# Moving an 80-word pad in SBUF: the weights start 192 bytes past a multiple of 512, the moving operands stay on it

## The chip, the cores and the metric

The kernel runs on one core of a Trainium2 chip. The metric is the device time of one execution in microseconds (us), taken as the median over runs.

## What is computed

Linear attention with a decay, then two feed-forward layers. All inputs are float32.

```
for t in range(S):                       # B, H, S, D = 4, 8, 768, 48
    state = alpha[:, :, t, :, None] * state + k_t (outer) v_t
    y[:, :, t] = q_t @ state
x = y as 3072 tokens x 384
x = ((x @ w_a) * (x @ w_b)) @ w_out      # d_ff = 1536
h = x @ w_in                             # d_ff = 2048
out = (max(h, 0) + alpha2 * min(h, 0)) @ w_out2
```

## The kernel before, in words

Every large product is made of three TensorE matmuls on operands that are split into a high and a low float32r part (high x high, low x high, high x low). The helper `mm3` (lines 931, 932 and 934) issues them. A matmul has a stationary operand, which a weight load (LDWEIGHTS) brings into the array, and a moving operand, which streams through it. In `mm3` the stationary operand is always a 128 x 128 piece of a weight tile: 512 bytes of each partition. The moving operand is 512 columns (2048 bytes of each partition), in the first block of tokens of the first unit 256.

The tokens are worked on in six blocks of 512. In the first layer `up` fills PSUM tiles `pa` and `pb` (moving `x`), a product and a split make `gh` and `gl`, and `down` adds into `acc` (moving `gh`, `gl`). In the second layer the PSUM tile of `up` is `pi`, and the weight tiles are called `v`. Attention chunks, 24 of them, stand between these matmuls in the first half. For the first four chunks TensorE has little else to do, and it is kept busy with throwaway bf16 matmuls (`wp`, line 343).

The order of all instructions comes from a planner (`Graph`), which works with a table of costs and due times. It knows no addresses, and it writes the instructions out engine by engine ahead of time.

Weights come from HBM as 64-bit numbers into a slot of the pool `wpool` and are turned there into the two float32r halves by ScalarE and VectorE (`conv`, lines 409 to 453). For three of the units the low half is found by TensorE (lines 481 to 483, tile `cl`): there the stationary operands are the constant matrices `plus` (+1 on the diagonal) and `minus` (-1), and the converted weights are the moving operand. The second layer's weights go back to HBM after conversion (`w2d`) and are loaded again as `v` tiles when slots are free. Chunks 2 and 3 of the attention keep their inputs `ra` and `kq` in weight slots that are not in use yet; chunks 0 and 1, and all later ones, keep them in the pool `tp`.

Where a tile lies in its partition is fixed when the program is built: pools lie one after the other in the order in which they are opened, and each is as large as its tiles. These are the bytes at which they start in the program before, and what is left of that when it is divided by 512 (its residue):

| pool, tiles | before: first byte, residue | after: first byte, residue |
|---|---|---|
| const: plus, minus, mask, betaT | 1152, 128 | 1152, 128 |
| pad of 80 words | 2752, 192 (end of const) | 125632, 192 (behind wpool) |
| wpool: 20 slots of 6144 bytes (weights; `vg`; `ra`, `kq` of chunks 2 and 3) | 3072, 0 | 2752, 192 |
| xpool: x | 125952, 0 | 125952, 0 |
| cpool: c1, c2 | 158720, 0 | 158720, 0 |
| gpool: a_sb, ng, gh, gl, x2 | 171008, 0 | 171008, 0 |
| tp: ra | 195584 and 199744, 0 and 64 | the same |
| tp: kq, v, ks; pers: Z, As, heads | 203904 and on, 128 | the same |

Every slot of wpool is 12 x 512 bytes long, and every piece that `mm3` takes as stationary operand starts a multiple of 512 bytes into its slot, so each has the residue of the pool. The 64-column pieces of `v` and `vg` in the attention are 256 bytes long: those of `v` start at residues 128 and 384, those of `vg` at 0 and 256. The operand of the throwaway matmuls starts 4 bytes into `heads`, at residue 132.

Of the kernel before, what the change touches and what calls it, by code (L numbers as in the profile page):

```python
# [14 lines left out]
F32 = mybir.dt.float32  # L15
# [10 lines left out]
P = 128  # L26
# [13 lines left out]
PAD = 80  # L40
# [259 lines left out]
def body(tc, akq, v, vg, w_a, w_b, w_o1, w_in, w_o2, beta, out):  # L300
# [13 lines left out]
    with ExitStack() as ctx:  # L314
        ctx.enter_context(tc.manual_schedule())
        pool = lambda name, bufs=1, **k: ctx.enter_context(tc.tile_pool(name=name, bufs=bufs, **k))
        const, wpool, xpool = pool("const"), pool("wpool"), pool("xpool", 2)
        cpool, gpool, tp, pers = pool("cpool", 2), pool("gpool", 2), pool("tp", 2), pool("pers")
        dram = pool("dram", space=DRAM)
        ps_mm, ps_acc = pool("ps_mm", 2, space=PSUM), pool("ps_acc", space=PSUM)  # L320
# [5 lines left out]
        ident = plus.bitcast(F32)  # L326
        mask = const.tile([P, P], F32, name="mask")
        betaT = const.tile([P, F2], F32, name="betaT")
        const.tile([P, PAD], F32, name="pad")
        Z = pers.tile([P, BC, NJ, D], F32, name="Z")  # L330
        At = pers.tile([P, NC + 2 * NJ * D + NC], F32, name="As")
        heads = pers.tile([P, NJ, CH + 1], F32, name="heads")
# [922 lines left out]
```

## Time and profile before

| | |
|---|---|
| median of 3 runs | 932.51 us (932.1 to 932.53) |
| the profiled execution's own time | 932.32 us |
| its span on the core | 930.6 us |
| TensorE busy (matmul) | 925.4 us, 6585 matmuls |
| weight loads busy | 757.0 us, 6585 loads |
| VectorE busy | 560.5 us |
| ScalarE busy | 242.6 us |
| mean granted TensorE clock | 1.0 of full |

The span is the time from the first to the last instruction on the core; the rest of the profiled execution's time lies around it. Records of matmuls overlap, since one starts while the one before still drains, so the time that one matmul costs is read from start to start and not from its own length.

### The profile page before, as it was taken

The page shows a single profiled execution, that of the slowest core. Times are in us where ns is not written, and L with a number is a line of the kernel's source. Part 1 is how long each engine was busy: PE and PEld are TensorE (multiplying, and loading weights), DVE is VectorE, ACT ScalarE, POOL GpSimd, SP SyncE. Part 2 cuts the span into 40 slices and gives each one's busy share as a digit, 9 for nine tenths or more (in the row PEclk, how much of TensorE's full clock was granted, in tenths as well). Part 3 has the DMA queues.
Part 4 walks back from the last instruction along what each step waited for, and adds up shares of the span by engine and source line. Part 5 has one row for each costly group of instructions (what it writes and reads, how often), then busy time and mean ns, then how long its engine had stood idle before and what let it go on. Part 6 is the DMA issues. An engine that isn't in the chain of part 4 may idle for free.

```text
span 930.6 us, 15550 instructions
## 1 busy us (share of the span) xinstructions
PE 925.4 (99%) x6585; PEld 757.0 (81%) x6585; DVE 560.5 (60%) x855; ACT 242.6 (26%) x396; POOL 7.0 (1%) x34
## 2 busy tenths in 40 slices
PE   9999999999999999999999999999999999999998
PEld 7887888888888888888888888888888888888886
DVE  8999996777668866532232254555545545555544
ACT  3555433333323332212222211111211111111211
POOL 0000000000000000000000000000000000000000
PEclk9999999999999999999999999999999999999999
DMA  9971256676748754430265610200200200200000
GB/s 363 402 282 51 89 159 199 185 217 213 225 136 260 234 159 141 116 92 22 77 236 203 236 70 1 83 19 1 98 5 1 101 1 1 102 1 0 35 1 35
DMA packets 75237, 112.89 MB, mean 121 GB/s; under 512 B 38688, under 2 KB 48416, under 8 KB 75168
## 3 DMA queue, kind: packets, MB, share of 16 engines
q1 hardware_dynamic: 75024, 111.77, 36.2%
q8 instruction: 52, 0.85, 0.4%
q14 instruction: 17, 0.14, 0.1%
q10 hardware_dynamic: 144, 0.13, 0.0%
HBM read 78.97 MB, written 30.93 MB: 118 GB/s over the span
## 4 chain that ended last, share of the span: by engine, by line
PE 97%; DVE 1%; DMA 1%; issue 1%; ACT 0%; DVEq 0%; ACTq 0%
PE acc L931 13%; PE acc L934 12%; PE acc L932 12%; PE pi L931 7%; PE pi L932 7%; PE pi L934 7%; PE pa L931 6%; PE pb L931 5%; PE pa L932 5%; PE pa L934 5%; PE pb L932 5%; PE pb L934 5%; PE both L791 2%; PE both L630 1%; PE both L813 1%; PE both L798 1%
## 5 line engine op out<-in xcount | busy, mean ns | idle before, releaser
L955 ACT CAST gh<-ng 128x512 fp32r<-128x512 f32 x96 | 59.7, 622 | 326.0 <-DVE ng L1168 251.3
L1164 DVE TENSOR_SCALAR ng<-pi,betaT 128x512 f32<-128x512 f32 x96 | 72.1, 751 | 97.1 <-PE pi L934 96.2
L959 DVE TENSOR_TENSOR gl<-ng,gh 128x512 fp32r<-128x512 f32 x96 | 66.3, 690 | 84.8 <-ACT gh L955 84.8
L1062 DVE TENSOR_TENSOR a_sb<-a_sb,pb 128x512 f32<-128x512 f32 (+1 forms) x74 | 49.5, 669 | 111.7 <-PE pb L934 110.8
L931 PE MATMUL pi<-x,v 128*128 128x512 f32 x288 | 112.8, 392 | 0.0
L932 PE MATMUL pi<-x,v 128*128 128x512 f32 x288 | 112.1, 389 | 0.0
L931 PE MATMUL acc<-gh,v 128*128 128x512 f32 x288 | 112.0, 389 | 0.0
L932 PE MATMUL acc<-gh,v 128*128 128x512 f32 x288 | 112.0, 389 | 0.0
L934 PE MATMUL acc<-gl,v 128*128 128x512 f32 x288 | 112.0, 389 | 0.0
L931 PE MATMUL acc<-gh,wo 128*128 128x512 f32 (+1 forms) x222 | 86.9, 391 | 0.0
L931 PE MATMUL pa<-x,wa 128*128 128x512 f32 (+1 forms) x222 | 86.6, 392 | 0.0
L931 PE MATMUL pb<-x,wb 128*128 128x512 f32 (+1 forms) x222 | 86.5, 391 | 0.0
L932 PE MATMUL acc<-gh,wo 128*128 128x512 f32 (+1 forms) x222 | 85.3, 384 | 0.0
L934 PE MATMUL acc<-gl,wo 128*128 128x512 f32 (+1 forms) x222 | 85.2, 384 | 0.0
L932 PE MATMUL pb<-x,wb 128*128 128x512 f32 (+1 forms) x222 | 85.0, 384 | 0.0
L932 PE MATMUL pa<-x,wa 128*128 128x512 f32 (+1 forms) x222 | 85.0, 384 | 0.0
L934 PE MATMUL pi<-x,v 128*128 128x512 f32 x288 | 80.9, 389 | 0.0
L955 ACT CAST gh<-a_sb 128x512 fp32r<-128x512 f32 (+1 forms) x74 | 45.1, 609 | 131.9 <-DVE a_sb L1062 124.0
L1059 ACT COPY a_sb<-pa 128x512 f32<-128x512 f32 (+1 forms) x74 | 42.5, 574 | 137.4 <-PE pa L934 137.2
L1168 DVE SCALAR_TENSOR_TENSOR ng<-pi,ng 128x512 f32<-128x512 f32 x96 | 66.3, 691 | 3.1
L931 PEld LDWEIGHTS pi<-x,v 128*128 128x128 f32 x288 | 54.0, 188 | 13.7 <-DVE ng L1168 2.6
L932 PEld LDWEIGHTS acc<-gh,v 128*128 128x128 f32 x288 | 54.1, 188 | 11.3
(122 smaller groups left out, 1343.7 us busy)
## 6 DMA issues: line engine op xcount, KB each, us to landing
kq<-in_akq SPq DMA_DIRECT2D x24, 512.0 KB, 5.1
w2d<-ws SPq DMA_DIRECT2D x16, 768.0 KB, 4.1
v<-w2d SPq DMA_DIRECT2D x16, 768.0 KB, 5.2
x2d<-x SPq DMA_DIRECT2D x18, 512.0 KB, 3.8
x<-x2d SPq DMA_DIRECT2D x6, 1536.0 KB, 7.2
ra<-in_akq SPq DMA_DIRECT2D x24, 258.5 KB, 3.0
v<-in_v SPq DMA_DIRECT2D x24, 256.0 KB, 5.2
rs<-in_w_in SPq DMA_DIRECT2D x8, 768.0 KB, 6.4
```

The costliest lines, as they stand in the source:

```text
L630: nc.tensor.matmul(a[hs, i, j, :], kT()[ps, j, hs], qT()[ps, j, hs], start=True, stop=True, skip_group_check=True)
L791: nc.tensor.matmul(y_of(k, half(p), part_of(h)), s["v"][part_of(h), 2 * j + i, :], s["As"][part_of(h), i, j, :], start=first, stop=False, ...
L798: nc.tensor.matmul(y_of(k, slice(64 * p, 64 * p + D), part_of(h)), z[ps, j, :], qT()[ps, j, part_of(h)], start=False, stop=last, skip_grou ...
L931: nc.tensor.matmul(o, lh, rh, start=first and n == 0, stop=False)
L932: nc.tensor.matmul(o, ll, rh, start=False, stop=False)
L934: nc.tensor.matmul(o, lh, rl, start=False, stop=last and n == len(pairs) - 1)
L955: nc.scalar.copy(gq[idx][0], src())
L959: nc.vector.tensor_tensor(out=gl, in0=src(), in1=gh.bitcast(F32), op=ALU.subtract)
L1059: nc.scalar.copy(b["a"], ba["t"])
L1062: nc.vector.tensor_tensor(out=b["a"], in0=b["a"], in1=bb["t"], op=ALU.mult)
L1164: nc.vector.tensor_scalar(out=b["n"], in0=bh["t"], scalar1=0.0, scalar2=betaT[:, i : i + 1], op0=ALU.min, op1=ALU.mult)
L1168: nc.vector.scalar_tensor_tensor(out=b["n"], in0=bh["t"], scalar=0.0, in1=b["n"], op0=ALU.max, op1=ALU.add)
```

## The change

One line of the pools and one line of the tiles. The pad leaves the pool `const` and gets a pool of its own, `gap`, that is opened between `wpool` and `xpool`. So wpool moves down by 320 bytes, from residue 0 to residue 192, and everything from xpool on stays where it was. On every engine, and in the DMA queues, the same instructions stand in the same order with the same shapes.

```
-        const, wpool, xpool = pool("const"), pool("wpool"), pool("xpool", 2)
+        const, wpool, gap, xpool = pool("const"), pool("wpool"), pool("gap"), pool("xpool", 2)
...
-        const.tile([P, PAD], F32, name="pad")
+        gap.tile([P, PAD], F32, name="pad")
```

## Rows read from the trace of the kernel before

**Rows 1.** The page's first two parts: busy time by engine, and 40 slices.

```profile
PE 925.4 (99%) x6585; PEld 757.0 (81%) x6585; DVE 560.5 (60%) x855; ACT 242.6 (26%) x396; POOL 7.0 (1%) x34
PE   9999999999999999999999999999999999999998
PEclk9999999999999999999999999999999999999999
DMA  9971256676748754430265610200200200200000
```

**Rows 2.** The chain that ended last, by engine; then a piece of it (start, us, what).

```profile
PE 97%; DVE 1%; DMA 1%; issue 1%; ACT 0%; DVEq 0%; ACTq 0%
...
27.11 5.85 DMA ra<-in_w_a
```

**Rows 3.** Groups by shape (count | busy us, mean ns | idle): first and last 512-wide matmul groups, loads.

```profile
L931 PE MATMUL pi<-x,v 128*128 128x512 f32 x288 | 112.8, 392 | 0.0
...
L934 PE MATMUL pa<-x,wa 128*128 128x512 f32 x210 | 59.0, 389 | 0.0
L932 PEld LDWEIGHTS pi<-x,v 128*128 128x128 f32 x288 | 54.1, 188 | 11.1
```

**Rows 4.** Timeline of TensorE and its loads in the second layer (start us, length us).

```profile
701.23 0.19 PEld L931 LDWEIGHTS pi<-x,v 128*128 128x128 f32 x1
701.45 0.39 PE L931 MATMUL pi<-x,v 128*128 128x512 f32 x1
701.45 0.19 PEld L932 LDWEIGHTS pi<-x,v 128*128 128x128 f32 x1
...
705.53 0.39 PE L931 MATMUL pi<-x,v 128*128 128x512 f32 x1
```

**Rows 5.** Timeline of TensorE: 256-wide `mm3` matmuls, and the throwaway ones.

```profile
24.87 0.28 PE L932 MATMUL pa<-x,wa 128*128 128x256 f32 x1
24.98 0.28 PE L931 MATMUL pa<-x,wa 128*128 128x256 f32 x1
25.10 0.28 PE L932 MATMUL pa<-x,wa 128*128 128x256 f32 x1
25.22 0.28 PE L931 MATMUL pa<-x,wa 128*128 128x256 f32 x1
...
10.77 1.58 PE L343 MATMUL wp<-heads 128*128 128x256 bf16 x13
```

**Rows 6.** Timeline of TensorE: the low half of weights (stationary plus, minus).

```profile
30.37 0.33 PE L483 MATMUL cl<-wb,plus 128*128 128x384 f32 x1
30.54 0.28 PE L931 MATMUL pb<-x,wb 128*128 128x256 f32 x1
```

**Rows 7.** Timeline of TensorE: scores of the first four chunks.

```profile
9.19 1.16 PE L620 MATMUL A<-kq 48*128 48x128 f32 x16
...
14.23 1.16 PE L620 MATMUL A<-kq 48*128 48x128 f32 x16
...
21.30 1.16 PE L620 MATMUL A<-kq 48*128 48x128 f32 x16
...
27.37 1.16 PE L620 MATMUL A<-kq 48*128 48x128 f32 x16
```

**Rows 8.** Timeline of TensorE: stationary `v`, then stationary `vg`.

```profile
15.83 0.84 PE L778 MATMUL both<-As,v 128*64 128x128 f32 x12
16.50 0.83 PE L782 MATMUL both<-As,vg 128*64 128x128 f32 x12
```

**Rows 9.** One line's instructions, VectorE (duration ns min/median/max, first and last start).

```profile
L603 DVE TENSOR_TENSOR kq<-kq,ra x24: 1199/1218/1228, 6.6 to 408.2; 128x1024 f32<-128x1024 f32 x24
```

**Rows 10.** Busy time by engine in a stretch (PE, PEld, DVE, ACT, POOL), clock, DMA share.

```profile
40.00:100.00 60.00, 60.00 (x651) 49.75 (x651) 59.95 (x101) 32.34 (x48) 0.65 (x3) 1.00 0.50 185
```

**Rows 11.** DMA issues (count, KB each, median us from issue to landing).

```profile
kq<-in_akq SPq DMA_DIRECT2D x24, 512.0 KB, 5.1
...
v<-w2d SPq DMA_DIRECT2D x16, 768.0 KB, 5.2
...
ra<-in_akq SPq DMA_DIRECT2D x24, 258.5 KB, 3.0
```

## The prediction

> **What bounds the kernel now.** I read the page's first two parts first: TensorE is busy for 925.4 of 930.6 us, in nearly every slice, at the full granted clock (2.4 GHz) [rows 1]. Then the chain that ended last: 97% of it is TensorE, 1% DMA, 1% VectorE [rows 2]. So the time is a number of matmuls times what one costs from start to start, and the view for that is the timeline. In the second layer the same matmul of `pi` comes again after 705.53 - 701.45 = 4.08 us, and 18 matmuls (nine of `up`, nine of `down`) lie in between: 0.2267 us each [rows 4]. 512 columns at 2.4 GHz are 0.2133 us, so a beat is the streaming of the moving operand and 0.0133 us more. The reader should also see when the weight loads run: a load starts at the same 701.45 at which the matmul before its own starts, takes 0.19 us by its record, and is over before the next start [rows 4]; the loads' own row has 11.1 us of idle time before 288 loads, some 39 ns each [rows 3].
>
> How many beats there are: six groups of 288 and nine of 210 matmuls, 512 wide, of which rows 3 show the first and the last: 1728 + 1890 = 3618, and 3618 x 0.2267 = 820 us of the span. 108 more are 256 wide. One nanosecond on every wide beat is 3.6 us. I count 0.2%, 1.9 us, as what a measurement of this kernel can tell from no change; that is 0.5 ns a beat, about one cycle of the full clock. So the question is narrow: does a stationary operand at residue 192 cost one cycle per matmul or none?
>
> **The change part by part.** No instruction is added, removed or moved. Three kinds of access get another address: weight loads (every matmul of `mm3`), VectorE and ScalarE work on the weight slots, and DMAs into and out of them. The pad itself is never touched.
>
> *Weight loads, for themselves.* A 512-byte piece at residue 0 lies within one stretch of 512 bytes, at residue 192 across two. If the load grew longer, would the beat? The narrow matmuls answer that: 256 columns start every 0.12 us (24.98, 25.10, 25.22), each with a full 128 x 128 load of its own [rows 5]. So loads can follow each other every 0.12 us, against 0.2267 us in a wide beat: some 0.1 us of cover, more than if a load took 1.8 times as long. Where the cover is gone, in the 108 narrow matmuls, a load 10% longer would cost 108 x 0.012 = 1.3 us. I take 0 for both.
>
> *Weight loads, against the moving stream.* The other way in is that the load, which reads SBUF while the matmul before it streams, holds up that stream at some pairs of addresses. The kernel before already has such pairs. Scores: chunks 0 and 1 have both operands at residue 128, chunks 2 and 3, in weight slots, at residue 0; all four groups of 16 last 1.16 us [rows 7]. To the 0.01 us of the rows that is at most 0.01/16 = 0.6 ns a matmul. Attention: pieces of `v` at 128 and 384, of which every second straddles a multiple of 512, against pieces of `vg` at 0 and 256, which never do: 0.84 and 0.83 us for 12 [rows 8], at most 0.01/11 = 0.9 ns, and the first of `v` stands behind other work. Float32r: the matmul of line 483 has a stationary operand at residue 128 and a moving one at 0. From its start to the next is 30.54 - 30.37 = 0.17 us for 384 columns [rows 6]; on the line between the narrow beat of 0.12 and the wide one of 0.2267, both of residue 0 throughout, it would be 0.173. And the throwaway bf16 matmuls, with both operands at 132, a residue that is a multiple of 4 alone, run one every (1.58 - 0.28)/12 = 0.108 us for 256 columns, against 0.1067 of streaming [rows 5] (0.28 us being about the length of one record). Nothing here depends on the residue of the stationary operand. What the rows do not have is residue 192 itself (64 past a multiple of 128) in float32r. So the value is 0, and the bounds are 0 and 0.9 ns x 3618 = 3.3 us; below nothing I let only the collision rival in.
>
> *VectorE and ScalarE on weight slots.* VectorE is full from 40 to 100 us, 59.95 of 60 [rows 10], so work that became slower there would have no cover. But the product of line 603 works on `kq` in weight slots for chunks 2 and 3 and in tp, at residue 128, for the others, and all 24 lie between 1199 and 1228 ns [rows 9]. I take 0; the whole spread, 2.4% of the 60 us, gives the upper bound of 1.4 us.
>
> *DMAs.* Weights are loaded before they are needed, and the chain waits for one of them only once, 5.85 us at 27.11 [rows 2]; that is the one place without cover. Loads to other residues land after 5.1 us for 512 KB (`kq`) and 3.0 us for 258.5 KB (`ra`, whose tile is loaded from its middle), loads of weights after 5.2 us for 768 KB [rows 11]: 10.0, 11.6 and 6.8 ns per KB. A fixed part explains that order, but taken as if it all came from the address it bounds the wait at 5.85 x 11.6/6.8 = 10.0 us, 4.1 us more. I take 0, since a start-up share of each DMA is the plainer reading.
>
> One rule speaks against the change here. The Trainium skill, "DMA: Bandwidth & Descriptors", section "How a descriptor splits into AXI transactions", says that a descriptor which does not start on a multiple of 256 bytes fetches bytes that it does not use. By it a 6144-byte row at residue 192 takes 198 beats in place of 192, 3% more; by that estimate the exposed wait would grow by 0.2 us, where the row's bound allows 4.1 us. No row here shows packets of both kinds.
>
> The sum: 0 + 0 + 0 + 0. The profiled execution took 932.32 us, 930.6 of it the span; the median of the runs is 932.51. I predict 932.4, between them.
>
> **The rivals.** *The load holds up the stream (slower).* At residue 192 a load reads from two 512-byte stretches while the matmul before streams, and each beat loses time. The place is every wide beat. One cycle of the 1.2 GHz level, 0.83 ns, is 3.0 us: 935.4 us; the bound of 0.9 ns gives 935.7. It decides from 0.5 ns a beat. For it speaks that residue 192 is in no row; against it all of rows 6, 7 and 8. 0.14.
>
> *Start-up gets slower (slower).* Either VectorE's work on slots, up to 1.4 us, or the exposed wait, up to 4.1 us: 932.4 + 4.1 = 936.5 at most. It decides when the wait grows by a third (1.9 of 5.85 us). The DMA rule named above is of this kind, and at its 3% it would leave the verdict at no change. 0.05.
>
> *The 13 ns are a collision of loads and stream at equal residues, and the move ends it (faster).* In the kernel before, weights and moving operands of `mm3` all have residue 0, and a narrow float32r beat is 0.12 us where a narrow bf16 one is 0.108 [rows 5]. If these 12 ns went away, 3726 matmuls would gain 44.7 us: 887.7 us; it decides from 0.5 ns. Against it: line 483 pairs residues 128 and 0, and still has 0.17 - 0.16 = some 0.01 us over its 384 columns [rows 6]. 0.06.
>
> Beside this rival stands what the Trainium skill says in "TensorE: Matmul & The Clock Gate", section "Back-to-back issue gap": a warm matmul follows the one before after its columns at 2.4 GHz and 2.5 ns. By it 512 columns would take 216 ns; the trace has 226.7 here, so the page does not explain the other 11 ns, and the measurement decides.
>
> **How the numbers follow.** No change 0.75, the held-up stream 0.14, start-up 0.05, collision ended 0.06. No change's own range is 931.5 to 933.3 (0.1% around 932.4). To hold 8 in 10 the range reaches up through the larger part of the slower cases to one 1.2 GHz cycle a beat and the VectorE bound's smaller part, 935.8; the faster rival is left out, so below it stays near the runs, 931.4. Faster by over 0.2%: 0.06. Slower: 0.14 + 0.05, of which a little stays under 1.9 us: 0.18. The rest, 0.76, is the same.
>
> **What would show it.** Right: the same `pi` matmul again after 4.08 us, 0.12 us narrow beats, loads of 188 ns, four equal score groups at 1.16 us with chunks 2 and 3 now at residue 192, line 603 within 1199 to 1228 ns, and a wait for `ra<-in_w_a` of about 5.85 us. The held-up stream would show as 4.09 us or more for 18 matmuls everywhere, whatever the DMAs do. A slower start would show as the same 4.08 us with all later work shifted by the same amount. The prediction is wrong if 192 differs from 128 for a float32r load: that is the one step that rests on residues which the rows do not contain.

## The result, and the profile after

The changed kernel takes 939.27 us (median of 6 runs, 938.82 to 939.78) against 932.31 us for the kernel before (6 runs beside it, 932.09 to 932.72): a ratio of 1.0073, 95% interval 1.0063 to 1.0083. That is 7 us slower, outside the range of the prediction. The profiled execution took 939.26 us.

The page of the changed kernel, first its span, then busy time by engine, then the chain that ended last:

```profile
span 937.5 us, 15550 instructions
...
PE 931.8 (99%) x6585; PEld 757.2 (81%) x6585; DVE 560.7 (60%) x855; ACT 242.4 (26%) x396; POOL 7.0 (1%) x34
...
PE 98%; DMA 1%; DVE 0%; ACT 0%; issue 0%; POOL 0%; ACTq 0%; POOLq 0%
```

The span grew by 6.9 us (from 930.6 us) and TensorE's busy time by 6.4 us, with the same 6585 matmuls. Loads, VectorE and ScalarE are busy as long as before to 0.2 us [rows 1]. So the matmuls take longer, and no other engine's work does. Where they cost more is read from start to start, as in [rows 4]. Timeline of TensorE in the second layer of the changed kernel (start us, length us):

```profile
702.23 0.39 PE L931 MATMUL pi<-x,v 128*128 128x512 f32 x1
702.46 0.39 PE L932 MATMUL pi<-x,v 128*128 128x512 f32 x1
702.69 0.39 PE L931 MATMUL pi<-x,v 128*128 128x512 f32 x1
702.92 0.39 PE L932 MATMUL pi<-x,v 128*128 128x512 f32 x1
...
704.29 0.39 PE L931 MATMUL acc<-gh,v 128*128 128x512 f32 x1
...
706.35 0.39 PE L931 MATMUL pi<-x,v 128*128 128x512 f32 x1
```

From 702.23 to 706.35 us there are 4.12 us for the 18 matmuls that took 4.08 us before: 0.2289 us a beat in place of 0.2267. Both layers have it as a mean (227.6 to 229.1 ns in the first, 226.8 to 228.9 in the second), though not each line of `mm3` by itself: the `acc` beats of the second layer went from 226.5, 227.0 and 226.5 ns (lines 931, 932, 934) to 227.4, 230.5 and 228.8. To the nanosecond the steady stretches have beats of 226, 229 and 232 ns, in a pattern that comes again after three, where there were only 226 and 227. The granted clock is no part of it (row of the windows view from 700 to 800 us; the 1.00 is the clock):

```profile
700.00:800.00 100.00, 100.00 (x438) 81.76 (x436) 51.95 (x74) 15.87 (x26) 0.00 (x0) 1.00 0.10 35
```

What did not move: the loads' own records (188 ns), the VectorE product on `kq`, whose chunks 2 and 3 now lie at residue 192, and the score groups of chunk 0 (residue 128) and chunk 2 (now 192), which answer to [rows 3, 9, 7]. (Chunk 1's group, whose tiles did not move, took 1.35 us; why is open.) The groups of loads, one line of VectorE, and the timeline of the scores in the changed kernel:

```profile
L932 PEld LDWEIGHTS pi<-x,v 128*128 128x128 f32 x288 | 54.1, 188 | 11.6
...
L603 DVE TENSOR_TENSOR kq<-kq,ra x24: 1197/1219/1228, 6.6 to 410.5; 128x1024 f32<-128x1024 f32 x24
...
8.66 1.16 PE L620 MATMUL A<-kq 48*128 48x128 f32 x16
...
21.22 1.16 PE L620 MATMUL A<-kq 48*128 48x128 f32 x16
```

**The sum of it.** 3618 wide beats times 2.2 ns are 8.0 us. All intervals between wide matmuls, added up one by one, lie 14.8 us above 226.67 ns each, where before they lay 8.3 us above it: 6.4 us more without rounding. The missing 1.6 us are beats behind pauses, which stand higher than the steady one in both kernels and less so in the changed one (the first three behind a pause: 233.3 ns before, 231.8 after).

Before the wide beats begin, 0.3 us are lost: the matmul of line 481 at 36.08 us now starts at 36.40. They are lost at 23 us, where TensorE waits for a load of `v` that it did not wait for before (23.04 us then):

```profile
23.38 0.67 PE L763 MATMUL dS<-v,ks 128*64 128x48 f32 x16 [0.34 <-DMA v<-in_v]
```

The chain's view puts 6.23 us to `ra<-in_w_a` in place of 5.85 [rows 2], but VectorE, which works on that tile, is busy through the whole 5.85 us of the kernel before, so that entry is no pause of its own. 6.4 and 0.3 make 6.7 of the 6.9 us.

### The profile page after: what moved, and what is told of

The parts are those of the page before. It is cut to its first block, busy times and chain, and to the rows that moved or that the text cites. A ratio compares the mean times of both kernels' runs of the same rounds, so it can differ in the third digit from the quotient of the medians.

```text
span 937.5 us, 15550 instructions
## 1 busy us (share of the span) xinstructions
PE 931.8 (99%) x6585; PEld 757.2 (81%) x6585; DVE 560.7 (60%) x855; ACT 242.4 (26%) x396; POOL 7.0 (1%) x34
## 4 chain that ended last, share of the span: by engine, by line
PE 98%; DMA 1%; DVE 0%; ACT 0%; issue 0%; POOL 0%; ACTq 0%; POOLq 0%
PE acc L931 13%; PE acc L932 12%; PE acc L934 12%; PE pi L931 7%; PE pi L934 7%; PE pi L932 7%; PE pa L931 6%; PE pb L931 5%; PE pa L932 5%; PE pa L934 5%; PE pb L932 5%; PE pb L934 5%; PE both L791 2%; PE both L630 1%; PE wp L343 1%; PE both L813 1%
```

## The experiments

In what follows *d* is the first byte of the moving operand less that of the stationary one, modulo 256. The kernel before has d = 0 in every `mm3` matmul (weights 0, moving operands 0), the changed one d = 64. Beats are means from start to start of 512-wide matmuls of the second layer, pauses left out.

### First question: what about the address is it?

Theory S: a stationary piece that straddles a multiple of 512 bytes costs. Theory M: one that starts off a multiple of 128 costs. Theory R: the stationary and the moving address cost when they are unequal, whatever each is. Four kernels move pools and nothing else; their edits are shown against the changed kernel. In each name the first number is the weights' residue, the second that of the moving operands.

**w192_x192**: no pad at all, so that the moving operands move by 320 bytes too.

```
-        const, wpool, gap, xpool = pool("const"), pool("wpool"), pool("gap"), pool("xpool", 2)
+        const, wpool, xpool = pool("const"), pool("wpool"), pool("xpool", 2)
...
-        gap.tile([P, PAD], F32, name="pad")
```

> No pad at all: weights and moving operands (x, gh, gl) all start at residue 192 of 512; tp and pers move from 128 to 320. Theory S (a 512-byte stationary piece that crosses a multiple of 512 costs the 2.2 ns a wide beat that the changed kernel shows, whatever the moving operand): 228.9 ns beats, some 939 us. Theory R (what costs is that stationary and moving operand differ in residue): 226.7 ns and 932.3 us, since they are equal here. Theory M (what costs is a start off a multiple of 128, of any operand): at least 228.9 ns, more if the moving operand pays too.

Measured: 932.83 us against 932.58, ratio 1.0004 (0.9994 to 1.0013). Timeline of its second layer (its lines stand two lower: L930 there is 932 here):

```profile
702.12 0.39 PE L930 MATMUL pi<-x,v 128*128 128x512 f32 x1
...
706.20 0.39 PE L930 MATMUL pi<-x,v 128*128 128x512 f32 x1
```

4.08 us for 18 matmuls, as in the kernel before. The weights lie exactly where they lie in the changed kernel, at 192, straddle multiples of 512 and start off multiples of 128, and cost nothing. S and M fall here.

**w0_x192**: the weights back at 0, the moving operands at 192.

```
-        gap.tile([P, PAD], F32, name="pad")
+        const.tile([P, 80], F32, name="pad")
+        gap.tile([P, 48], F32, name="pad2")
```

> The mirror image of the change: weights at residue 0, x, c1, gh, gl at 192, tp and pers at 320. Theory S: 226.7 ns beats, 932.3 us, since no stationary piece crosses a multiple of 512. Theory R: 228.9 ns, some 939 us, since the residues differ by 192 as in the change. Theory M: slower than 226.7 ns if a moving operand off a multiple of 128 pays, else 226.7.

Measured: 953.51 us, ratio 1.0226 (1.0211 to 1.0242), 233.3 ns a beat. The weights that were free in the kernel before are now dearer than in the changed one.

**w128_x0**: weights at 128, by `betaT` and an 80-word pad behind wpool.

```
-        betaT = const.tile([P, F2], F32, name="betaT")
-        gap.tile([P, PAD], F32, name="pad")
+        betaT = gap.tile([P, F2], F32, name="betaT")
+        gap.tile([P, 80], F32, name="pad2")
```

> Weights at residue 128, all from x on as before (betaT lies behind the weights). Theory S: 228.9 ns, some 939 us, since each stationary piece crosses a multiple of 512. Theory R: slower than 226.7 ns too, by an amount that need not be the same. Theory M: 226.7 ns and 932.3 us, since 128 is a multiple of 128.

Measured: 951.25 us, ratio 1.0200 (1.0185 to 1.0216), 232.5 ns a beat. Timeline of its second layer (lines one lower):

```profile
706.68 0.39 PE L930 MATMUL pi<-x,v 128*128 128x512 f32 x1
...
710.87 0.39 PE L930 MATMUL pi<-x,v 128*128 128x512 f32 x1
```

4.19 us. A multiple of 128 is no better than 192 but worse.

**w256_x0**: weights at 256, where every 512-byte piece straddles a multiple of 512.

```
-        mask = const.tile([P, P], F32, name="mask")
+        mask = gap.tile([P, P], F32, name="mask")
-        gap.tile([P, PAD], F32, name="pad")
+        const.tile([P, 16], F32, name="pad")
+        gap.tile([P, 64], F32, name="pad2")
```

> Weights at residue 256, all from x on as before (mask lies behind the weights). Theory S: 228.9 ns, some 939 us. Theory R: slower than 226.7 ns. Theory M: 226.7 ns and 932.3 us. If 128 and 256 differ from each other, the cost goes with the residue by degrees, and none of the three holds as it stands.

Measured: 932.50 us, ratio 1.0000 (0.9990 to 1.0010). Timeline of its second layer:

```profile
701.64 0.39 PE L931 MATMUL pi<-x,v 128*128 128x512 f32 x1
...
705.72 0.39 PE L931 MATMUL pi<-x,v 128*128 128x512 f32 x1
```

4.08 us. Straddling is free once more, and 256 is as good as 0. R as it was put down missed here too: it asked for a cost, since 256 and 0 are unequal. It holds only for addresses taken modulo 256, and no shorter period will do, since 128 against 0 costs.

### Second question: how does the cost go with d?

Theory P: the price hangs on d alone (then weights at 320 and moving at 0 must cost what w0_x192 did, both d = 192), in its simplest form the more the farther d is from 0, or in steps of 64 bytes. Theory Q: each residue has a price of its own.

**w320_x0, w224_x0, w160_x0, w352_x0**: d = 192, 32, 96 and 160, by `mask` behind wpool and pads of other sizes in front of it and behind it. The first of them:

```
-        mask = const.tile([P, P], F32, name="mask")
+        mask = gap.tile([P, P], F32, name="mask")
-        gap.tile([P, PAD], F32, name="pad")
+        const.tile([P, 32], F32, name="pad"); gap.tile([P, 48], F32, name="pad2")
```

w224_x0 and w352_x0 have pads of 8 and 72, and of 40 and 40 words there; w160_x0 has 8 and 72 and `betaT` behind wpool too.

> Weights at residue 320, all from x on at 0 as before, so moving minus stationary is 192 modulo 256, as with weights at 0 and x at 192. Theory P (only the difference modulo 256 counts, because a load is read while the matmul before it streams): wide beats of 233.3 ns and 953.5 us, as there. Theory Q (each operand's own residue has a price of its own, and that of the moving operand was what made weights at 0, x at 192 slow): not above the 951 us that weights at 128 took, since the moving operand is at 0.

> Weights at 224: moving minus stationary is 32 modulo 256. Theory P with a cost that grows with the overlap: between the 0 at difference 0 and the 7 us at 64, some 3 us, 935 to 936 us. Theory P with steps of 64 bytes: like difference 0 (932.3) or like 64 (939.3).

> Weights at 160: difference 96. Theory P with a growing cost: between 939.3 (64) and 951.3 (128), some 945 us. In steps of 64 bytes: like 64 (939.3) or like 128 (951.3).

> Weights at 352: difference 160. Theory P with a growing cost: between 951.3 (128) and 953.5 (192), some 952 us. In steps of 64 bytes: like one of the two.

Measured (medians; two executions each of these four kernels), with the runs of before:

| kernel | d | us | ratio to before (95%) | beat, ns |
|---|---|---|---|---|
| before, w192_x192, w256_x0 | 0 | 932.3 to 932.8 | 1.000 | 226.8 |
| w224_x0 | 32 | 954.09 | 1.0229 (1.0199 to 1.0259) | 233.3 |
| after | 64 | 939.27 | 1.0073 (1.0063 to 1.0083) | 228.9 |
| w160_x0 | 96 | 954.33 | 1.0232 (1.0202 to 1.0261) | 233.3 |
| w128_x0 | 128 | 951.25 | 1.0200 (1.0185 to 1.0216) | 232.5 |
| w352_x0 | 160 | 957.30 | 1.0264 (1.0234 to 1.0293) | 234.3 |
| w320_x0 | 192 | 953.65 | 1.0224 (1.0195 to 1.0254) | 233.3 |
| w0_x192 | 192 | 953.51 | 1.0226 (1.0211 to 1.0242) | 233.3 |

Timeline of the second layer of w352_x0, the slowest:

```profile
706.67 0.39 PE L931 MATMUL pi<-x,v 128*128 128x512 f32 x1
...
710.88 0.39 PE L931 MATMUL pi<-x,v 128*128 128x512 f32 x1
```

4.21 us. Timelines of the two kernels with d = 192, w0_x192 and then w320_x0:

```profile
703.55 0.39 PE L931 MATMUL pi<-x,v 128*128 128x512 f32 x1
...
707.75 0.39 PE L931 MATMUL pi<-x,v 128*128 128x512 f32 x1
...
703.90 0.40 PE L931 MATMUL pi<-x,v 128*128 128x512 f32 x1
...
708.10 0.40 PE L931 MATMUL pi<-x,v 128*128 128x512 f32 x1
```

4.20 us in both, and the whole kernels agree to 0.14 us, although one moved the weights and the other everything else: P holds in that, and Q falls. The cost does not grow with d, though, nor go in steps of 64: 32 costs three times what 64 does, and the forecasts for d = 32, 96 and 160 (932 to 954 us) each lay below what was measured. Both simple forms of P fall. The change happened to land on the mildest of the unequal values tried.

### Third question: only the address, and whose beat pays

The four kernels from here on were executed once each; what is compared lies within one execution.

**fine1**: pools as in the kernel before. In the second layer alone the stationary piece starts *r* bytes past a multiple of 512 inside the same tile (the high half's r bytes later, the low half's 512 - r bytes earlier), with another r in each of twelve stretches of eight half-units. Theory P says that each stretch has its own beat, by r; rival T says that it is where tiles lie, what the DMAs and the other engines do, and that all stretches stay at 226.7 ns.

```
+PAD = 80; OFFS = [(0, 0), (1, 1), (4, 4), (6, 6), (12, 12), (16, 16), (20, 20), (28, 28), (32, 32), (48, 48), (56, 56), (80, 80)]
...
+        def shifted(r, f, s): h, l = OFFS[s]; h0, l0 = f + h, UC + f + (l - P if l else 0); return r[:, h0 : h0 + P], r[:, l0 : l0 + P]
```

> All tiles where they were before; in the second layer the stationary pieces (high and low half alike) begin 0, 4, 16, 24, 48, 64, 80, 112, 128, 192, 224 and 320 bytes past a multiple of 512, in twelve stretches of some 32 us one after the other, so the second layer's values are not the reference's. Theory P (the address of the load against that of the stream counts, modulo 256): 226.7 ns in the first stretch, 233.3 at 64 and at 320 (as with weights at 320), 232.5 at 128, 228.9 at 192 (as in the changed kernel), 233.3 at 224, and values between 226.7 and 234.3 elsewhere. Rival T (where the tiles, the DMAs or VectorE's slots lie is what costs, not the piece's start): 226.7 ns in all twelve.

Measured, mean beat in ns by r in bytes: 0: 227.0; **4: 232.4**; 16: 233.4; 24: 230.0; 48: 233.3; 64: 233.3; 80: 232.0; 112: 233.3; 128: 233.3; **192: 228.9**; 224: 233.3; 320: 233.3. Timeline of the same kernel, `pi` of one half-unit and of the next, in the stretches of r = 0, 4, 192 and 224:

```profile
535.00 0.39 PE L931 MATMUL pi<-x,v 128*128 128x512 f32 x1
...
539.09 0.39 PE L931 MATMUL pi<-x,v 128*128 128x512 f32 x1
...
566.02 0.40 PE L931 MATMUL pi<-x,v 128*128 128x512 f32 x1
...
570.20 0.39 PE L931 MATMUL pi<-x,v 128*128 128x512 f32 x1
...
834.78 0.39 PE L931 MATMUL pi<-x,v 128*128 128x512 f32 x1
...
838.90 0.39 PE L931 MATMUL pi<-x,v 128*128 128x512 f32 x1
...
867.82 0.39 PE L931 MATMUL pi<-x,v 128*128 128x512 f32 x1
...
872.02 0.39 PE L931 MATMUL pi<-x,v 128*128 128x512 f32 x1
```

4.09, 4.18, 4.12 and 4.20 us for the same 18 matmuls of one run. T falls: tiles, slots and DMAs stayed as they were, and the start address of the piece changes the beat by itself. Here d is -r modulo 256: r = 192 is d = 64 and gives the 228.9 ns of the changed kernel, r = 224 is d = 32, r = 64 and 320 agree, and 4 bytes are enough. (At r = 128 it is 0.8 ns more than in w128_x0.)

**mixed**: the same kernel, but the high and the low piece get residues of their own, so that loads with d = 0 and loads with d unequal 0 alternate. Theory L: the beat pays in which an unequal load runs (while the matmul before it streams). Theory O: the beat pays whose own weights are unequal.

```
+PAD = 80; OFFS = [(0, 0), (0, 32), (32, 0), (32, 32), (0, 16), (16, 0), (16, 16), (0, 56), (56, 0), (56, 56), (0, 0), (64, 64)]
```

> As fine1, but the high and the low half get residues of their own: (high, low) = (0,0), (0,128), (128,0), (128,128), (0,64), (64,0), (64,64), (0,224), (224,0), (224,224), (0,0), (256,256) bytes; the second layer's values are not the reference's. Line 931 has a high piece, line 932 a low one, line 934 a high one. Theory L (the load for the next matmul collides with the stream of the present one): with (0,128) the time from a start of line 931 to the next of line 932 is longer, the others stay at 226.7; with (128,0) it is the two others that are longer. Theory O (a matmul is slow by its own stationary operand's address): with (0,128) the time from a start of line 932 to the next start is longer. (256,256) gives 226.7 throughout if the period is 256.

Measured, mean beat by residues (high, low): (0, 0) 227.0 and 227.2; (256, 256) 226.7; (0, 128) 231.2; (128, 0) 233.1; (128, 128) 232.4; (0, 64) 230.9; (64, 0) 232.6; (64, 64) 233.3; (0, 224) 231.2; (224, 0) 233.0; (224, 224) 233.4. Line 932 alone has the low piece as its weights. Timeline in the stretch (0, 128):

```profile
570.20 0.40 PE L931 MATMUL pi<-x,v 128*128 128x512 f32 x1
...
573.67 0.40 PE L931 MATMUL acc<-gh,v 128*128 128x512 f32 x1
573.90 0.40 PE L932 MATMUL acc<-gh,v 128*128 128x512 f32 x1
574.14 0.39 PE L934 MATMUL acc<-gl,v 128*128 128x512 f32 x1
574.36 0.40 PE L931 MATMUL pi<-x,v 128*128 128x512 f32 x1
```

The 18 matmuls take 4.16 us, 0.08 more than with equal residues, for six unequal loads: 13 ns each. By line, to the nanosecond: the beat of line 931, in which the unequal load runs, takes 232.3 ns; the beat of 932, whose own weights they are, 234.2 to 234.5; those of 934 keep 226.5 to 227.0. In the stretch (0, 224) it is 235.0, 231.5 to 231.8 and 226.5 to 226.7; in (0, 64) it is less clean, 228.7, 234.3 and 229.3. So one unequal load costs in the beat of its load and in that of its use, and neither L nor O is right alone; when every load is unequal, the costs do not add up, and it is 5.7 to 6.7 ns a beat.

### Fourth question: is it the amount that is loaded, or the type?

**width**: the second layer again, now with the loads narrowed to W columns, but for the first and the last of each group. Theory C: the cost goes with the columns loaded; rival A: any unequal load costs the same.

```
+WID = [128, 128, 64, 32, 96, 128, 64, 32, 96, 96, 64, 32]
...
+                W = w[0] if w else P; nc.tensor.matmul(o if n == 0 else o[0:W], lh if n == 0 else lh[:, 0:W], rh, start=first and n == 0, stop=False)
+                nc.tensor.matmul(o[0:W], ll[:, 0:W], rh, start=False, stop=False)
```

> As fine1, but in the second layer every weight load except the first and the last of a group takes only so many columns of its piece. Stretches (residue, columns): (0,128), (64,128), (64,64), (64,32), (64,96), (112,128), (112,64), (112,32), (112,96), (0,96), (0,64), (0,32); rows of the output that these columns would have made are left out, so the second layer's values are not the reference's. Theory C (words that the load reads collide with words that the stream reads): the 6.7 ns that a beat has over 226.7 at residues 64 and 112 shrink with the columns, to some half at 64 and a quarter at 32 columns, where only narrow loads follow each other (from line 934 to 934, and from 931 to 932 and back after the first). Rival A (an unequal start costs a fixed time per load): 233.3 ns at every width. At residue 0 both expect 226.7 or less.

Measured, ns by W = 128, 96, 64, 32: residue 0: 227.0, 230.7, 229.9, 230.8; residue 64: 233.4, 230.0, 233.0, 231.4; residue 112: 233.3, 230.1, 232.9, 231.8. Timeline in the stretch of residue 64 and W = 32:

```profile
641.76 0.39 PE L931 MATMUL pi<-x,v 128*128 128x512 f32 x1
...
645.93 0.39 PE L931 MATMUL pi<-x,v 128*128 128x512 f32 x1
```

4.17 us, against 4.20 with whole loads. This decides nothing: the cost does not shrink with W, as C has it, nor stay, as A has it, and loads of mixed width are slower at equal residues too (229.9 to 230.8), so that a fast beat to compare with is missing.

**bf16**: the second layer's `acc` matmuls read both operands as bf16 (pieces of 256 bytes, r from 0 to 256) and `pi` stays float32r at residue 0. Theory F: only float32r pays.

```
+        def shifted(r, f, s, half): ...; z = r.bitcast(BF16); return (z[:, 2 * h0 : 2 * h0 + P], z[:, 2 * l0 : 2 * l0 + P]) if half else (r[:, h0 : h0 + P], r[:, l0 : l0 + P])
```

> In the second layer the down matmuls (acc) read bfloat16 operands, 128 stationary columns in 256 bytes and 512 moving columns in 1024, the stationary ones from the bits of the weight tiles at residues 0, 4, 16, 32, 64, 96, 112, 128, 160, 192, 224 and 256 of 512 in twelve stretches; up stays float32r at residue 0. The second layer's values are not the reference's. Theory F (only float32r loads, 512 bytes in 188 ns, collide): one beat of acc in all twelve stretches, near the 0.108 us of 256 columns of the throwaway matmuls, so some 0.216 us for 512. Theory G (any load against any stream): longer beats of acc at residues that are not a multiple of 256, by an amount that need not be that of float32r.

Measured: 215 to 216 ns (median) in all twelve stretches. Timeline in the stretch r = 96:

```profile
709.98 0.38 PE L931 MATMUL acc<-gh,v 128*128 128x512 bf16 x1
709.98 0.10 PEld L932 LDWEIGHTS <-v 128*128 128x128 bf16 x1
710.20 0.38 PE L932 MATMUL acc<-gh,v 128*128 128x512 bf16 x1
...
710.41 0.38 PE L934 MATMUL acc<-gl,v 128*128 128x512 bf16 x1
...
710.63 0.38 PE L931 MATMUL acc<-gh,v 128*128 128x512 bf16 x1
...
711.28 0.19 PEld L932 LDWEIGHTS pi<-x,v 128*128 128x128 f32 x1
```

0.65 us for three. The address plays no part for these bf16 matmuls, and F holds. (bf16 also halves the bytes of load and stream; type and bytes were not taken apart.) The bf16 load takes 0.10 us, the float32r one 0.19.

## Why the prediction was wrong

**The step that failed** is "Weight loads, against the moving stream", taken as 0 with an upper bound of 0.9 ns a beat. It is 2.2 ns (d = 64), so what the rival "the load holds up the stream" forecast, a longer wide beat in both layers, happened, above the price that the prediction gave it: 939.3 us, not 935.4 to 935.7. Its reason, two stretches of 512 bytes, was wrong: w256_x0 straddles them and is free. What counts is the difference of the two addresses, shown by w192_x192 (same weights, no cost) and by fine1 (same tiles, cost by r).

**Why the rows did not warn.** The prediction looked for controls by the residue of the stationary operand. In most of them the moving operand had moved along. The scores read both operands from one tile `kq`, so d = 0 in all four groups [rows 7], and the throwaway matmuls read both from `heads` [rows 5]. The matmuls on `v` have d = 0 and those on `vg` d = 128 [rows 8], so that row did compare an equal with an unequal pair, but in plain float32 with 64-column loads. In that form unequal addresses cost nothing: from the first start of a `vg` group to the eleventh it is 545 to 547 ns in the kernel before, the changed one and all eight kernels that move pools, with d from 0 (w128_x0) to 224 (w160_x0). One row had the right pair: line 483, float32r, stationary at 128, moving at 0 [rows 6]. It was read as 0.17 us beside an interpolated 0.173, and the 0.01 us of the row is coarser than the 6 ns in question (to the nanosecond the four intervals of this line are 168 to 179, a spread that hides as much). So the 0.9 ns were a bound for other cases. The sentence "The prediction is wrong if 192 differs from 128 for a float32r load" looked at the weights alone as well: 128 against 0 costs even more than 192 against 0.

**The collision rival** looked at the right quantity, the two residues together, with the sign turned round for the wide beats: equal residues are the cheapest case there is here, not the cause of the 13 ns. bf16, at 2.5 ns over its columns, shows that these come with the float32r form. (In the 108 narrow beats the sign is the rival's: 120 ns at d = 0, 115.5 and 115.9 at d = 192; that is worth 0.5 us at most.)

**Weight loads, for themselves**: right. The records stayed at 188 ns, and w192_x192 has weights at 192 at no cost. The 256-wide beats, where cover was feared to be short, even fell from 120 to 118 ns.

**VectorE and ScalarE on slots**: right, with line 603 between 1197 and 1228 ns. **DMAs**: right to the size of the measurement, 0.3 us, though the one exposed wait was misread: what grew is the wait for `v`, not the chain's entry for `ra<-in_w_a`. w256_x0 has the matmul of line 481 at 36.37 us, 0.3 later too, and still ends at 932.5; w0_x192, with weights at 0, has it at 35.89. The Trainium skill's rule of 256 bytes for descriptors ("DMA: Bandwidth & Descriptors", "How a descriptor splits into AXI transactions") put 0.2 us on it at residue 192, by the prediction's estimate; but weights at 256, where it asks for nothing, show the same shift, and bf16, with weights at 0, waits 0.17 us for `v` too, so no run here shows its effect.

**Clock, count of beats, bound**: right. 3618 beats at full clock decide the time, which is why 2.2 ns became 7 us.

The Trainium skill has a sentence against the mechanism that happened: "Loading the next tile's weights doesn't steal SBUF read bandwidth from the running matmul" ("TensorE: Matmul & The Clock Gate", "Step-by-step: what each phase is for"). For bf16 the runs agree, 215 to 216 ns at every address. For float32r the beat does depend on where the weights lie: 227.0 to 233.4 ns for the same matmul, by the start of the weights alone (fine1); whether read bandwidth is what is lost was not shown.

**What stays open.** That the load and the stream get in each other's way at unequal addresses is the reading of mixed, where one unequal load costs in the beat of its load and in the beat of its use. Which resource they share was not shown: width, the run meant for it, came out between its theories. Why d = 64 (and 232, r = 24) is milder than its neighbours is open too. Nor is d = 0 enough for the fast beat: in the kernel before the first three beats behind a pause take 233.3 ns, the next six 229.3 to 229.9, and only then 226.7; and `pi` at d = 0 takes 229.8 on average where it alternates with bf16 groups (bf16), and the beats 229.9 to 230.8 where load widths are mixed (width). What lets it settle was not looked for. No version that computes the same beat the kernel before; d = 0 is the best of all that were tried, and w192_x192 has it without a pad.

## What to carry to other kernels

Where float32r matmuls with whole 128-column loads follow each other back to back, let stationary and moving operands start at equal addresses modulo 256 bytes; here everything else that was tried cost 1 to 3% of a 512-wide beat, and a pad that serves one pool can break the match with another. When rows are used as controls for an address, write down the address of both operands of each row, and ask in which of them the thing that the change alters, here a difference, was ever unequal. A bound from rows holds for their case only, type and pairing included.

## What the runs showed of the hardware

- The 512-wide float32r beat depends on (moving less stationary start) modulo 256: 226.8 ns at 0, 228.9 at 64, 230.0 to 234.3 at all others tried, 4 bytes apart included; two pairs of different addresses with d = 192 agree to 0.14 us in 953. Several values of d give the same 233.3 ns; at 2.4 GHz that is 560 cycles, where 226.7 ns are 544.
- After a pause the equal-address beat is not fast at once: 233.3 ns for the first three, 226.7 from the tenth on (kernel before).
- Plain float32 matmuls of 128 columns with 64-column loads (`vg`) take the same time at seven values of d, 545 to 547 ns for ten intervals.
- The 256-wide beat goes the other way: 120 ns at d = 0, 115.5 to 119.9 at unequal d (115.5 and 115.9 at d = 192). It was not followed up.
- bf16 with the same shapes takes 215 to 216 ns at every address, and its load 97 to 98 ns beside 188.
- Narrowing some of the float32r loads at d = 0 made the beats slower, 229.9 to 230.8 ns, though the narrow loads' own records were shorter (108, 134 and 161 ns at 32, 64 and 96 columns beside 188 at 128).
